# The last 16 rows of the first query weights in 31 small loads behind the first K load

## The chip, the cores and the metric

The kernel runs on one core of a Trainium2 chip. The metric is the device time of one execution in microseconds (us), as the median of several runs. A core has compute engines (TensorE for matrix products, written PE in the profile; VectorE, DVE; ScalarE, ACT; GpSimd, POOL), a queue engine that issues most of the transfers here (SyncE, SP), and 16 DMA engines that carry them out.

## The reference

One decode step of a transformer block in float32, for one token of width 512. Layer norm, 32 query heads over 8 key/value heads, a cache of 65536 positions of 128 values for each of the 8, the output projection, then a bilinear feed-forward layer of width 1792.

```python
q = (layernorm(x) @ wq).reshape(1, 1, 32, 128)          # 4 query heads for each K/V head
scores = einsum(q, repeat(k_cache, 4)) * 128 ** -0.5
o = einsum(softmax(scores), repeat(v_cache, 4))
h = x + o.reshape(1, 1, 4096) @ wo
n = layernorm(h)
out = h + ((n @ w_gate) * (n @ w_up)) @ w_down
```

The K and V caches are 537 MB of the 565 MB that the kernel reads.

## The kernel before

The work goes head by head over the 8 K/V heads (`h`). For each head the kernel needs its query weights and its output weights (512 x 512 each, both in the tile `wqo_sb`, 16 KB in each of the 128 partitions), four K blocks and four V blocks of 8.39 MB. A block is 128 partitions of 64 KB, and lies in one of two buffers, `kv[0]` and `kv[1]`, which the blocks use in turn (`buf`).

TensorE runs one loop over the heads (`head`, line 333): 16 matmuls for the query projection (L336), four K blocks of 32 matmuls (L346), the softmax with its transposes (L352 to L364), four V blocks of 32 matmuls (L374), and the projection of the output (L381, L387). A float32 matmul shows as two instructions. After the loop comes the feed-forward layer: gate and up (L409), down (L439).

SP issues all the large loads in a fixed order, written out for the eight heads. Before each K or V load from the third on it waits until TensorE has finished with the block before last, whose buffer the load takes (`done[-2]`, L132). So at most two blocks are loaded or waiting for use. The weights of the next head are loaded ahead of the third V block (L137). The weights of the first head are the first load of the program (L127, from the array `wq0`, 128 rows of 8 KB), and raise the semaphore `s_wq` by 16. TensorE waits for that semaphore once, before the loop (L331):

```python
sp.dma_start(wq_sb, wq0).then_inc(s_wq, 16)      # L127
...
take(s_wq, 16)                                   # L331
```

In the list of instructions `kv0` and `kv1` are the two buffers, `wqo_sb` the weights, `psc0` a bank of scores, `sm0` a bank for small results. ACT issues two small loads of `x` at the start (L124, L125). The last V block and the feed-forward weights come in pieces (L143, L153 to L160), and the output of 4 rows of 512 B is written at the end (L313).

Of the kernel before, what the change touches and what calls it, by code (L numbers as in the profile page):

```python
# [24 lines left out]
P = 128  # L25
# [6 lines left out]
KT = D // P  # L32
# [6 lines left out]
PE_ONLY = bass.OrderedEngineSet([mybir.EngineType.PE])  # L39
V_CUTS = (0, 16, 24, 28, 32)  # L40
U_CUTS = (0, 2, 3, 4)
D_CUTS = (0, 6, 10, 12, 13, 14)


# [15 lines left out]
def body(nc, xc, xr, kT, v, wq0, wqo, wo7, wg, wu, wd, out):  # L60
    pe_e, dve_e, act_e, pool_e, sp = nc.tensor, nc.vector, nc.scalar, nc.gpsimd, nc.sync

    def tile(name, *shape):
        return nc.alloc_sbuf_tensor(name, list(shape), F32).ap()
# [5 lines left out]
    wqo_sb = tile("wqo_sb", P, 2, KT, 512)  # L70
    wq_sb, wo_sb = wqo_sb[:, 0], wqo_sb[:, 1]
# [32 lines left out]
    def sem(name):  # L104
        sems.append(nc.alloc_semaphore(name))
        return sems[-1]
# [4 lines left out]
    s_wq, s_w = sem("s_wq"), sem("s_w")  # L111
    s_vp = [sem(f"s_vp{i}") for i in range(len(V_CUTS) - 1)]
    s_wg = sem("s_wg")
    s_wu = [sem(f"s_wu{i}") for i in range(len(U_CUTS) - 1)]
    s_wd = [sem(f"s_wd{i}") for i in range(len(D_CUTS) - 1)]
    s_x, s_xr, s_out = sem("s_x"), sem("s_xr"), sem("s_out")
# [3 lines left out]
    def pe_at(h, m):  # L120
        return M_HEAD * h + m
# [2 lines left out]
    act_e.dma_start(x_col, xc).then_inc(s_x, 16)  # L124
    act_e.dma_start(x_row, xr).then_inc(s_xr, 16)  # L125

    sp.dma_start(wq_sb, wq0).then_inc(s_wq, 16)  # L127
    done = []
    for h in range(HKV):
        for i in range(2 * NT):  # L130
            if len(done) >= 2:
                sp.wait_ge(pe.sem, done[-2])  # L132
            buf = len(done) % 2
            if i == NT + 2:
                sp.wait_ge(pe.sem, pe_at(h, M_Q))
                if h < LAST:
                    sp.dma_start(wqo_sb, wqo[h]).then_inc(s_w, 16)  # L137
                else:
                    sp.dma_start(wo_sb, wo7).then_inc(s_w, 16)
            if h == LAST and i == 2 * NT - 1:  # L140
                for p, (lo, hi) in enumerate(zip(V_CUTS, V_CUTS[1:])):
                    cs = slice(lo * 512, hi * 512)
                    sp.dma_start(kv[buf][:, cs], v[h, i - NT][:, cs]).then_inc(s_vp[p], 16)  # L143
            else:
                src = kT[h, i] if i < NT else v[h, i - NT]
                whole = i == 2 * NT - 1
                sp.dma_start(kv[buf], src).then_inc(s_vp[0] if whole else s_kv[buf], 16)
                for p in s_vp[1:] if whole else ():

                    sp.sem_inc(p, 16)  # L150
            done.append(pe_at(h, M_K + i if i < NT else M_V + i - NT))
    sp.wait_ge(pe.sem, pe_at(LAST, M_V + 2))
    sp.dma_start(wg_t, wg).then_inc(s_wg, 16)  # L153
    for p, (lo, hi) in enumerate(zip(U_CUTS, U_CUTS[1:])):
        cs = slice(lo * F, hi * F)
        sp.dma_start(wu_t[:, cs], wu[:, cs]).then_inc(s_wu[p], 16)
    sp.wait_ge(pe.sem, pe_at(LAST, M_V + 3))
    for p, (lo, hi) in enumerate(zip(D_CUTS, D_CUTS[1:])):
        cs = slice(lo * D, hi * D)
# [141 lines left out]
    for half in range(2):  # L301
        cs = slice(half * 256, min(FJ, half * 256 + 256))
# [19 lines left out]
    def take(s, n=1):  # L322
        pe_e.wait_ge(s, n).then_inc(s, -n)  # L323
# [4 lines left out]
    pe_e.wait_ge(dve.sem, c_s2)  # L328
    mm(sm[1][:, 0:1], mean_m, ln_s2, start=True, stop=True).then_inc(pre, 1)
    pe_e.wait_ge(dve.sem, c_const)  # L330
    take(s_wq, 16)  # L331

    def head():
        for r in range(REP):
# [66 lines left out]
    def project(acc, w, sems):  # L401
        for k in range(KT):
            if len(sems) == 1 and k == 0:
                pe_e.wait_ge(sems[0], 16)
            elif len(sems) > 1 and k in U_CUTS:
                pe_e.wait_ge(sems[U_CUTS.index(k)], 16)
            for j in range(4):
# [24 lines left out]
    for c in range(NC):  # L432
        if c == 8:
            pe_e.wait_ge(dve.sem, c_fp1)
        if c in D_CUTS:
            pe_e.wait_ge(s_wd[D_CUTS.index(c)], 16)
        for j in range(4):
# [46 lines left out]
```

## Time and profile before

| | us |
|---|---|
| median of 3 runs (1312.80 to 1312.94) | 1312.81 |
| the profiled execution, its own time | 1313.45 |
| its span, first to last instruction | 1312.1 |
| TensorE matmuls busy | 717.8 |
| TensorE weight loads busy | 249.1 |
| VectorE busy | 73.3 |
| ScalarE busy | 47.2 |

The mean granted clock of TensorE is 0.732 of full speed. The span is what the rows of the trace cover, and lies 1.35 us below the execution's own time. An engine's busy time is a sum over its instructions; what matters for the time is which wait ends last. For loads there are three views: the page gives the share of the 16 DMA engines' time that each queue took; a table by stretches of time gives share and GB/s; and the timeline gives the starts of matmuls, which wait for loads. In the queues' rows q1 is that of SP's transfers, q10 that of ACT's, q8 and q14 are the loads of instructions.

### The profile page before, as it was taken

The numbers are of one execution on the slowest core, as the hardware profiler recorded it, in microseconds if no ns is written. First come the engines' busy times: TensorE is split into PE (matmuls) and PEld (weight loads), VectorE is DVE, ScalarE is ACT, GpSimd is POOL, SyncE is SP. The second block draws the span as 40 slices with busy tenths as digits, with TensorE's granted clock in tenths as the row PEclk, the third lists the DMA queues.
The fourth block names the chain that finished last, engine by engine and source line by source line (L and its number), as shares of the span: only waits on it lengthen the run. The fifth ranks groups of instructions, "written<-read, shape, count | busy, mean of one in ns | idle before, by whom it ended". The sixth has DMA issues, their size and how long they took to land. (4 is left out here: it accounts for less than half of the span.)

```text
span 1312.1 us, 10526 instructions
## 1 busy us (share of the span) xinstructions
PE 717.8 (55%) x4922; PEld 249.1 (19%) x4922; DVE 73.3 (6%) x180; ACT 47.2 (4%) x102; POOL 2.5 (0%) x13
## 2 busy tenths in 40 slices
PE   4355374553755446563574736735465454645657
PEld 3011031210312112120131201312121111211213
DVE  0000000100001000010000100001000010000101
ACT  0010000100001000010000100001000010000100
POOL 0000000000000000000000000000000000000000
PEclk9777676786767867767767767668677677777677
DMA  9999999999999999999999999999999999999998
GB/s 416 436 424 446 422 440 424 440 424 440 440 428 442 426 438 426 438 428 438 440 428 440 428 438 426 438 428 438 438 432 436 430 422 441 438 428 438 438 414 356
DMA packets 12405, 564.80 MB, mean 430 GB/s; under 512 B 1510, under 2 KB 1514, under 8 KB 2155
## 3 DMA queue, kind: packets, MB, share of 16 engines
q1 hardware_dynamic: 12248, 564.67, 99.6%
q8 instruction: 6, 0.10, 0.0%
q10 hardware_dynamic: 146, 0.00, 0.0%
q14 instruction: 5, 0.03, 0.0%
HBM read 564.66 MB, written 0.00 MB: 430 GB/s over the span
## 5 line engine op out<-in xcount | busy, mean ns | idle before, releaser
L346 PE MATMUL psc<-kv,q_pad 128*32 128x512 f32 x2048 | 296.8, 744 | 257.0 <-PEq L323 257.0
L374 PE MATMUL pva<-kv,pt 128*16 128x512 f32 x2048 | 283.1, 714 | 272.9 <-PEq L323 272.7
L346 PEld LDWEIGHTS psc<-kv,q_pad 128*32 128x32 f32 x2048 | 81.6, 133 | 465.7 <-issue 465.7
L374 PEld LDWEIGHTS pva<-kv,pt 128*16 128x16 f32 x2048 | 67.5, 111 | 492.0 <-issue 492.0
L224 ACT COPY sc<-psc 128x512 f32<-128x512 f32 x32 | 18.8, 586 | 1146.2 <-PE psc L346 1146.2
L230 DVE TENSOR_REDUCE mx<-sc 128x1 f32<-128x512 f32 x32 | 21.9, 686 | 541.2 <-ACT sc L224 541.2
L336 PE MATMUL sm<-xn,wqo_sb 128*128 128x1 f32 x256 | 48.8, 325 | 2.2 <-issue 2.2
L336 PEld LDWEIGHTS sm<-xn,wqo_sb 128*128 128x128 f32 x256 | 48.1, 293 | 9.6 <-issue 9.6
L264 DVE COPY orow<-pva 128x512 f32<-128x512 f32 x8 | 5.5, 692 | 566.6 <-PE pva L374 566.6
L361 PE MATMUL ptp<-ident,sc 128*128 128x128 f32 x128 | 29.2, 395 | 10.2 <-PEq L323 9.7
L361 PEld LDWEIGHTS ptp<-ident,sc 128*128 128x128 f32 x128 | 21.3, 201 | 15.5 <-issue 14.8
L249 ACT ACTIVATE sc<-sc,nbias 128x512 f32<-128x512 f32 x32 | 22.7, 711 | 20.2 <-DVE nbias L244 20.2
L254 DVE COPY pt<-ptp 128x512 f32<-128x512 f32 x32 | 22.1, 692 | 21.5 <-PE ptp L361 21.5
L366 PE MATMUL pva<-zeros 128*32 128x512 f32 x64 | 13.8, 948 | 0.0
L387 PE MATMUL attn<-wqo_sb,o_pad 128*32 128x512 f32 x64 | 10.9, 756 | 3.3 <-PEq L323 3.3
L381 PE MATMUL sm<-sel_b,orow 128*128 128x4 f32 x64 | 8.2, 252 | 7.2 <-PEq L323 7.2
L381 PEld LDWEIGHTS sm<-sel_b,orow 128*128 128x128 f32 x64 | 7.7, 191 | 14.4 <-issue 14.4
L352 PE MATMUL sm<-ident,m 128*1 128x128 f32 x8 | 2.2, 269 | 13.7 <-PEq L323 13.7
L364 PE MATMUL sm<-l,ones 128*128 128x4 f32 x16 | 4.1, 324 | 9.6 <-PEq L323 9.6
L409 PE MATMUL psc<-kv,hn_pad 128*32 128x448 f32 x64 | 8.9, 702 | 0.6 <-DMA kv<-in_wu 0.3
L439 PE MATMUL pva<-kv,f_pad 128*32 128x128 f32 x112 | 6.1, 416 | 1.1 <-DMA kv<-in_wd 1.1
L354 PE MATMUL sm<-ones,mexp 1*128 1x1 f32 x16 | 3.3, 276 | 5.7 <-PEq L323 5.7
(83 smaller groups left out, 67.7 us busy)
## 6 DMA issues: line engine op xcount, KB each, us to landing
wqo_sb<-in_wqo SPq DMA_DIRECT2D x7, 2048.0 KB, 14.0
kv<-in_v SPq DMA_DIRECT2D x1, 4096.0 KB, 22.5
kv<-in_wg SPq DMA_DIRECT2D x1, 3584.0 KB, 18.0
kv<-in_v SPq DMA_DIRECT2D x1, 2048.0 KB, 27.0
kv<-in_v SPq DMA_DIRECT2D x2, 1024.0 KB, 30.0
kv<-in_wu SPq DMA_DIRECT2D x1, 1792.0 KB, 22.4
kv<-in_wu SPq DMA_DIRECT2D x2, 896.0 KB, 24.9
kv<-in_wd SPq DMA_DIRECT2D x1, 1536.0 KB, 20.1
```

The costliest lines, as they stand in the source:

```text
L224: copies.append(act.tick(act_e.copy(sc[s], psc[s % 2])))
L230: i = dve_e.tensor_reduce(out=mx[:, s:s + 1], in_=sc[s], axis=AX.X, op=ALU.max)
L249: act_e.activation(sc[s], sc[s], AF.Exp, bias=nbias[:, 0:1], scale=SCALE, accum_out=sums[:, s:s + 1]).then_inc(atok, 1)
L254: dve_e.tensor_copy(pt[s].rearrange("p g b h -> p b g h"), ptp[s % 2].rearrange("p (b g h) -> p b g h", b=4, h=REP)).then_inc(tok, 1)
L336: i = mm(sm[0][:, r:r + 1], wq_sb[:, k, r * P:(r + 1) * P], xn[:, k:k + 1], start=(k == 0), stop=(k == KT - 1))
L346: i = mm(psc[s % 2][32 * j:32 * j + 32, :], q_pad[:, 28 - 4 * rs:60 - 4 * rs], kv[s % 2][:, (4 * rs + j) * 512:(4 * rs + j + 1) * 512], st ...
L361: i = pe_e.transpose(ptp[s % 2][:, b * P:(b + 1) * P], sc[s][:, b * P:(b + 1) * P], ident)
L366: mm(pva[32 * j:32 * j + 32, :], zeros[:, 0:32], zeros, start=True, stop=False)
L374: i = mm(pva[32 * j:32 * j + 16, :], pt[n][:, 8 * j + rs, :, :].rearrange("p b h -> p (b h)"), vt[:, w * 512:(w + 1) * 512], start=False, ...
L381: i = mm(sm[0][:, 0:REP], orow[:, b * P:(b + 1) * P], sel_b[:, 4 * b:4 * b + 4], start=(b == 0), stop=(b == 3))
L387: i = mm(attn[32 * r:32 * r + 32, :], o_pad[:, r, :], wo_sb[:, r, :], start=True, stop=True)
L409: i = mm(acc[32 * j:32 * j + 32, :FJ], hn_pad[:, k, :], w[:, o:o + FJ], start=(k == 0), stop=(k == KT - 1))
```

## The change

The first load now brings rows 0 to 111 of the query weights. Rows 112 to 127 come in 31 loads that SP issues right behind the first K load. They go through the 2048 columns in steps of 128 (512 B of a row): in step r, from 1 to 15, one load brings the first r of the 16 rows and another the other 16-r; the last load brings the last 128 columns of all 16 rows. TensorE waits for all of them at the same place as before, for the sum of 32 loads (512).

```diff
+STEP = 128
...
-    sp.dma_start(wq_sb, wq0).then_inc(s_wq, 16)
+    flat = wqo_sb.rearrange("p a k c -> p (a k c)")
+    n_wq = 0
+    for lo, hi in ((0, P - 16),):
+        sp.dma_start(wq_sb[lo:hi], wq0[lo:hi]).then_inc(s_wq, 16)
+        n_wq += 16
...
                 sp.dma_start(kv[buf], src).then_inc(s_vp[0] if whole else s_kv[buf], 16)
                 for p in s_vp[1:] if whole else ():
                     sp.sem_inc(p, 16)
+                if not done:
+                    wq0_flat = wq0.rearrange("p k c -> p (k c)")
+                    for r in range(1, 16):
+                        cs = slice((r - 1) * STEP, r * STEP)
+                        for lo, hi in ((P - 16, P - 16 + r), (P - 16 + r, P)):
+                            sp.dma_start(flat[lo:hi, cs], wq0_flat[lo:hi, cs]).then_inc(s_wq, 16)
+                            n_wq += 16
+                    cs = slice(15 * STEP, KT * 512)
+                    sp.dma_start(flat[P - 16:, cs], wq0_flat[P - 16:, cs]).then_inc(s_wq, 16)
+                    n_wq += 16
...
-    take(s_wq, 16)
+    take(s_wq, n_wq)
```

On SP, at the start of the program, the loads stood like this before:

```order
L127 DMA wqo_sb<-in_wq0 128x2048 [waits barrier_Pool_Activation_PE_DVE_SP_release]
L147 DMA kv0<-in_kT 128x16384
L147 DMA kv1<-in_kT 128x16384
L147 DMA kv0<-in_kT 128x16384 [waits pe]
L147 DMA kv1<-in_kT 128x16384 [waits pe]
```

At the same place they now stand like this, the middle of the small loads left out:

```order
L133 DMA wqo_sb<-in_wq0 112x2048 [waits barrier_Pool_Activation_PE_DVE_SP_release]
L154 DMA kv0<-in_kT 128x16384
L163 DMA wqo_sb<-in_wq0 1x128
L163 DMA wqo_sb<-in_wq0 15x128
L163 DMA wqo_sb<-in_wq0 2x128
...
L163 DMA wqo_sb<-in_wq0 15x128
L163 DMA wqo_sb<-in_wq0 1x128
L166 DMA wqo_sb<-in_wq0 16x128
L154 DMA kv1<-in_kT 128x16384
L154 DMA kv0<-in_kT 128x16384 [waits pe]
L154 DMA kv1<-in_kT 128x16384 [waits pe]
```

Between the loads of `kv0` and `kv1` stand 31 small ones, and the wait of the third K load has not moved against its neighbours.

On TensorE, at the entry of the loop, the changed program reads:

```order
L346 MATMUL sm1<-ln_s2,mean_m 128x1 [waits dve,pool]
L408 UNCONDITIONAL_BRANCH [waits s_wq,dve]
L408 BRANCH_PREFETCH_HINT
L353 MATMUL sm0<-xn,wqo_sb 128x1 x16
L363 MATMUL psc0<-kv0,q_pad 32x512 [waits tok,s_kv0]
```

This order is that of before but for line numbers: the wait on `s_wq` stands ahead of the query projection and the first K block, and now counts loads that are queued behind that K block's own.

## Rows read from the trace of the kernel before

**Rows 1.** The page: DMA busy tenths in 40 slices; queues (packets, MB, share); bytes read.

```profile
DMA  9999999999999999999999999999999999999998
...
q1 hardware_dynamic: 12248, 564.67, 99.6%
q8 instruction: 6, 0.10, 0.0%
...
HBM read 564.66 MB, written 0.00 MB: 430 GB/s over the span
```

**Rows 2.** Busy time by stretch: 200 to 300 us, with DMA share and GB/s.

```profile
core 0: us, PE busy (x) PEld busy (x) DVE busy (x) ACT busy (x) POOL busy (x), PEclk, DMA share, GB/s
200.00:300.00 100.00, 52.28 (x349) 15.44 (x349) 6.10 (x14) 4.69 (x11) 0.00 (x0) 0.72 1.00 433
```

**Rows 3.** Timeline of TensorE: query projection and K blocks of heads 1, 2 and 8.

```profile
start us, us, engine line op out<-in xcount [idle before <-releaser]
10.40 6.97 PE L336 MATMUL sm<-xn,wqo_sb 128*128 128x1 f32 x32 [2.19 <-issue]
25.15 9.32 PE L346 MATMUL psc<-kv,q_pad 128*32 128x512 f32 x64 [7.78 <-PEq L323]
45.89 9.20 PE L346 MATMUL psc<-kv,q_pad 128*32 128x512 f32 x64 [11.42 <-PEq L323]
65.40 9.68 PE L346 MATMUL psc<-kv,q_pad 128*32 128x512 f32 x64 [10.31 <-PEq L323]
84.76 8.54 PE L346 MATMUL psc<-kv,q_pad 128*32 128x512 f32 x64 [9.68 <-PEq L323]
...
186.26 8.99 PE L346 MATMUL psc<-kv,q_pad 128*32 128x512 f32 x64 [1.72 <-PEq L323]
205.61 9.55 PE L346 MATMUL psc<-kv,q_pad 128*32 128x512 f32 x64 [10.37 <-PEq L323]
225.11 10.03 PE L346 MATMUL psc<-kv,q_pad 128*32 128x512 f32 x64 [9.96 <-PEq L323]
...
1144.45 9.46 PE L346 MATMUL psc<-kv,q_pad 128*32 128x512 f32 x64 [1.70 <-PEq L323]
1163.80 10.02 PE L346 MATMUL psc<-kv,q_pad 128*32 128x512 f32 x64 [9.89 <-PEq L323]
```

**Rows 4.** DMA packets and queues that start in 25 to 44 us, then 63 to 82.

```profile
DMA packets 140, 8.21 MB, mean 432 GB/s; under 512 B 14, under 2 KB 14, under 8 KB 14
q1 hardware_dynamic: 139, 8.19, 99.7%
q8 instruction: 1, 0.02, 0.3%
...
DMA packets 145, 8.41 MB, mean 442 GB/s; under 512 B 16, under 2 KB 16, under 8 KB 16
q1 hardware_dynamic: 144, 8.39, 102.1%
```

**Rows 5.** The chain of waits that ended last: start us, us, what.

```profile
1283.72 20.06 DMA kv<-in_wd
1303.78 0.14 issue
1303.91 6.12 PE pva L439 x112
1310.03 0.02 issue
1310.06 0.29 DVE y L311
```

**Rows 6.** DMA packets and queues of 1311.5 to 1311.8 us, the output.

```profile
DMA packets 8, 0.00 MB, mean 7 GB/s; under 512 B 4, under 2 KB 8, under 8 KB 8
q1 hardware_dynamic: 8, 0.00, 3.0%
```

**Rows 7.** The same of 1307.5 to 1308.5 us, the last rows of 2 KB.

```profile
DMA packets 37, 0.06 MB, mean 61 GB/s; under 512 B 7, under 2 KB 7, under 8 KB 37
q1 hardware_dynamic: 37, 0.06, 16.1%
```

**Rows 8.** Timeline of the issues, by SP and ACT.

```profile
0.74 0.39 SPq L127 DMA_DIRECT2D wqo_sb<-in_wq  x1
1.18 0.55 ACTq L125 DMA_DIRECT2D x_row<-in_xr  x1
1.19 0.41 SPq L147 DMA_DIRECT2D kv<-in_kT  x1
34.53 0.33 SPq L147 DMA_DIRECT2D kv<-in_kT  x1
...
1283.72 2.23 SPq L160 DMA_DIRECT2D kv<-in_wd  x5
1310.38 0.65 SPq L313 DMA_DIRECT2D out_y<-y  x1
```

**Rows 9.** Busy time by stretch, as rows 2, at the first bytes.

```profile
1.00:1.75 0.75, 0.00 (x0) 0.00 (x0) 0.15 (x2) 0.00 (x0) 0.58 (x2) 1.00 0.00 0
1.75:1.90 0.15, 0.00 (x0) 0.00 (x0) 0.00 (x0) 0.15 (x1) 0.15 (x2) 1.00 4.27 601
```

**Rows 10.** The loads of line 147: from issue to landing; first is shortest, second longest.

```profile
DMA to landing us min/median/max: 23.8/29.5/44.1
```

## The prediction

> **What bounds the kernel now.** I read the page's slices and queues first. The queue of the loads, q1, took 99.6% of the 16 DMA engines' span, and the DMA row is 9 in every slice but the last [rows 1]. So the kernel reads memory from start to end, and everything that an engine computes lies beside it. Next comes the pace. From 200 to 300 us the engines moved 433 GB/s at a busy share of 1.00 [rows 2], that is 27.06 GB/s each. The timeline of TensorE gives the same pace in loads: the K blocks of a head start 19.35 us apart (186.26 and 205.61; 1144.45 and 1163.80) [rows 3], and 8.39 MB in 19.35 us is 433.5 GB/s. The pace of the second head is that of the eighth. A block's matmuls take 8.5 to 10.0 us of those 19.35, so TensorE waits for loads, never the other way.
>
> One interval is longer: the first K block starts at 25.15 and the second at 45.89, 20.74 us later, 1.39 us over the pace [rows 3]. In that stretch the instruction queue q8 shows one packet of 0.02 MB beside the loads [rows 4]. From 63 to 82 us there is such a packet too (145 packets, 144 of them of q1 [rows 4]), yet the blocks of 65.40 and 84.76 are 19.36 apart [rows 3]. I read this so: an instruction fetch takes one DMA engine away from its loads for a while. A load counts as landed when its last engine is done. So the first fetch, which puts one engine behind the other 15, costs time, and a later one, which puts another engine behind by no more, costs none. **The end is set by the engine that is furthest behind.** At the end the chain of waits goes through the first down-projection load to 1303.78, then 6.12 us of matmuls, then the output [rows 5]. A shift of the last engine goes through to the end one for one.
>
> **The change, part by part.** *Taken away:* the last 16 rows of the first query weights as part of the first load, one row of 8 KB for each engine: 8192 B at 27.06 GB/s are 0.30 us less for every engine.
>
> *Added:* 31 loads behind the first K load. Steps of r and 16-r rows (r from 1 to 15) cover 128 columns each, a last one all 16 rows. That is 256 pieces of 512 B, the same bytes. I take it that a load of r rows gives one row to each of the first r engines. The one load of before with few rows fits: the output of 4 rows shows 8 packets, 4 of them under 512 B [rows 6], so four pieces with four completions. Then engine e (0 to 15) gets 31-2e pieces: 31 the first, 1 the last, 16 on average.
>
> *Price of a piece:* the 8 packets of the output took 3.0% of 16 engines for 0.30 us, 0.144 us, or 36 ns for a piece with its completion [rows 6]. That is a store, and mine are loads, so bounds: from below the bytes alone, 512 B at 27.06 GB/s = 19 ns; from above a row of four times the size, the 2 KB rows near the end, where 30 rows with 7 completions took 16.1% of 16 us = 2.58 us, under 86 ns each [rows 7]. I take 36, from the row of the same size. The first engine then gains 31 x 36 - 300 = +0.81 us (+0.29 to +2.4 by the bounds), the last 36 - 300 = -0.27 us, the mean +0.27. That is the stagger: 1.08 us between first and last, after the first K load, and it stays, as each queue then holds equal shares.
>
> *What the stagger buys in the long stretch:* nothing that a row shows. The stretch runs at 433 GB/s with all engines busy, and at an unchanged pace. The 1.39 us lost near the start are spread among engines in another way, not saved.
>
> *The end, then:* it moves by what the engine that is last gains. If that is the one which the first fetch hit, it lies between -0.27 and +0.81. No row names it. Several engines are hit (q8 has 6 packets [rows 1]), and the latest of several is likelier to be one with many pieces, so I take the upper part, **+0.6 us**.
>
> *Issue on SP:* 31 more instructions stand between the first and the second K load. A load of 128 rows takes 0.33 to 0.45 us (five in 2.23 us); the two loads of few rows took 0.55 (on ACT) and 0.65 (SP) [rows 8]. I take 0.65: first K issued until 1.60, 31 x 0.65 = 20.2, second K issued at 21.8. Bytes flow 1.0 us after an issue begins (0.74 to 1.75 [rows 8, 9]), so at 22.8. What hides it: the first K load lands at 1.19 + 23.8 = 25.0 [rows 10], and the pieces keep the first engine busy to about 25.8. The cover is 3.0 us; the price is nil at 0.65, and 31 us for each us of an issue above (25.8 - 1.0 - 1.6) / 31 = 0.75.
>
> *The wait of TensorE:* it now waits for all 512 counts before the first head, and so for pieces that land behind the first K load, near 25.8 and not 5. The query projection, 6.97 us, and the first K block, 9.32 [rows 3], come one after the other: 25.9 + 7.0 + 0.4 + 9.3 = 42.6. SP waits for that block before the third K load, now issued at 42.6 and not at 34.53 [rows 8], with bytes at 43.6. The second K load, which landed at 45.8 (1.6 + 44.1 [rows 8, 10]), keeps the last engine busy to about 46.4. The cover falls from 11 us to near 2.8 us, and it holds; without it each us of delay is one at the end. ScalarE and VectorE only wait longer, and are back in step by the second block at about 46.5.
>
> **A rule against the stagger.** The trace shows loads back to back at the pace of their bytes: the 8.39 MB loads 19.35 us apart [rows 3]. The Trainium skill ("DMA: Bandwidth & Descriptors", section "Rules for kernel authors") says that transfers under 64 KB pay mostly overhead and are better put together; its section "Anatomy of one DMA" gives about 2 us as the fixed part, for a load issued from GpSimd. Were that 2 us paid in turn by each of the 31 small loads, the sum by it would be 62 us, an estimate: 1374 us. The trace speaks against it, as the output's four pieces kept four engines busy for 36 ns each.
>
> **Rivals.**
> 1. *SP is too slow with the small loads* (slower). A small load would have to keep SP for over 0.75 us; the end moves by 31 times the excess. At 0.85: +0.6 + 3.2, 1316.6 us. For it: 0.65 is already twice the 0.33 of a large load, and no row shows 33 loads queued at once (SP may also have to stop until some have drained). Against: 0.65 leaves 3.0 us.
> 2. *A piece costs an engine more than 36 ns* (slower). Each 10 ns more are 0.31 us on the first engine. At the 86 ns of a 2 KB row +2.4: 1315.2; at 120 ns 31 x 0.12 - 0.3 = +3.4: 1316.2. For it: a load, not a store, and a completion behind each 512 B. Against: bytes a quarter of the 86 ns row.
> 3. *The change does not do what it says*: a load of few rows is carried by one engine. That engine has 256 x 36 ns - 0.3 = +8.9 us: 1321.7. Against it is the output with its four completions. The Trainium skill ("DMA: Bandwidth & Descriptors", section "Why a DMA increments its semaphore by 16 and not by 1") agrees: the number of engines is the largest up to 16 that divides the rows, the lowest-numbered ones.
> 4. *The 1.39 us near the start are a collision of engines in step, not the fetch*, and the stagger takes them away: 1312.8 - 1.4 = 1311.4. For it: it comes at the first interval only, when all engines have just begun together. Against: the fetch lies in the same stretch [rows 4].
> 5. *Engines in step slow each other through the whole run.* Then the pace of 19.35 us would fall; 0.1 us off each of some 67 such loads (564.67 MB / 8.39 [rows 1]) is 6.7 us: 1306. Against: 433 GB/s from the second head to the last without change, though fetches had moved engines apart by then. The Trainium skill (the same page, section "Latency and other measured facts") has copies of lock-stepped rows at large powers of two falling to half rate or less; there the sum would be far more, but no stretch here is that slow.
>
> **How the numbers follow.** The profiled run is 1313.45 with a span of 1312.1, 1.35 around it; the median of the runs is 1312.81, 0.64 below the profiled run. The shift is added to the median: 1312.81 + 0.6 = **1313.4 us**. Chances: this forecast 0.79 (alone 1312.5 to 1313.6, and to 1315.2 at the upper bound of a piece); rival 4 0.04; rival 1 0.08; rival 2 beyond its bound 0.04; rival 3 0.02; rival 5 0.03. The range takes in the forecast, the upper bound of a piece and rival 4: 1311.3 to 1315.2. Within 0.2% (2.6 us, about what a measurement of this kernel can tell from no change) are the forecast and rival 4: 0.83. Slower are rivals 1 to 3: 0.14. Faster is rival 5: 0.03.
>
> **What the profile of the changed kernel would show.** Right: the first head's query projection starts near 26 us, the first K block near 33, the second near 46.5; SP begins the second K load before 24 and the third before 44; later K blocks 19.35 us apart; 256 packets of 512 B more, and no stretch before 1280 us with a DMA share below 0.9. Wrong: a second K load issued after 24.8 (rival 1); a block pace other than 19.35 (rival 5); a second K block before 45.5 (rival 4) or beyond 48 with SP in time (rivals 2 and 3).

## The result and the profile after

| | before | after |
|---|---|---|
| median of 6 runs, us | 1312.85 (1312.72 to 1312.94) | 1319.18 (1318.98 to 1319.32) |
| ratio | | 1.0048 (95% interval 1.0038 to 1.0058) |
| span of the profiled execution | 1312.1 | 1317.9 |

The change costs 6.3 us. The forecast was 1313.4, with a range that ended at 1315.2. The page of the changed kernel gives the queues as [rows 1] do:

```profile
DMA  9999999999999999999999999999999999999998
...
q1 hardware_dynamic: 12744, 564.67, 99.6%
q8 instruction: 6, 0.10, 0.0%
...
HBM read 564.66 MB, written 0.00 MB: 428 GB/s over the span
```

The bytes are the same, and 496 more packets run on q1: 256 pieces with a completion each are 512, and the first load lost 16 rows. A slice of this page is 33 us wide, too wide to show a hole. The timeline of TensorE shows where the time went; its rows answer to [rows 3] (first the query projection, then K blocks of heads 1 and 8):

```profile
31.75 6.98 PE L353 MATMUL sm<-xn,wqo_sb 128*128 128x1 f32 x32 [24.20 <-PEq L340]
39.23 9.26 PE L363 MATMUL psc<-kv,q_pad 128*32 128x512 f32 x64 [0.50 <-PEq L340]
50.13 7.07 PE L363 MATMUL psc<-kv,q_pad 128*32 128x512 f32 x64 [1.64 <-PEq L340]
70.65 8.92 PE L363 MATMUL psc<-kv,q_pad 128*32 128x512 f32 x64 [13.45 <-PEq L340]
90.97 9.00 PE L363 MATMUL psc<-kv,q_pad 128*32 128x512 f32 x64 [11.39 <-PEq L340]
...
1151.15 9.68 PE L363 MATMUL psc<-kv,q_pad 128*32 128x512 f32 x64 [1.68 <-PEq L340]
1170.51 8.54 PE L363 MATMUL psc<-kv,q_pad 128*32 128x512 f32 x64 [9.68 <-PEq L340]
```

Against before the second block starts 4.24 us later (50.13 for 45.89), the third 5.25 (70.65 for 65.40), the fourth 6.21 (90.97 for 84.76), the first two of the last head 6.70 (1151.15 for 1144.45) and 6.71. So nearly all is lost in the first 91 us, and the long stretch keeps the pace of 19.36. The query projection starts at 31.75, where 25.9 was forecast.

The loss stays up to the last projection, whose matmuls start 6.52 us later (1310.43 for 1303.91). The spans of the two profiled executions differ by only 5.8, because these matmuls ran at different granted clocks (PEclk, third number from the end; first before, then after):

```profile
1303.90:1310.00 6.10, 6.08 (x112) 5.69 (x112) 0.00 (x0) 0.00 (x0) 0.00 (x0) 0.52 0.54 210
...
1310.40:1312.00 1.60, 1.52 (x48) 1.28 (x48) 0.00 (x0) 0.00 (x0) 0.00 (x0) 1.00 1.01 407
```

Before, all 112 ran back to back near the lower of the two levels (1.2 GHz) and ended 6.12 us after their start. In the changed kernel they ran at the upper one (2.4 GHz), waited for their loads in between, and ended 0.47 us after the last start. Why the levels differ was not tried.

The issues on SP, the counterpart of [rows 8]:

```profile
1.20 0.42 SPq L154 DMA_DIRECT2D kv<-in_kT  x1
1.67 10.19 SPq L163 DMA_DIRECT2D wqo_sb<-in_wq  x30
11.90 0.32 SPq L166 DMA_DIRECT2D wqo_sb<-in_wq  x1
12.26 0.45 SPq L154 DMA_DIRECT2D kv<-in_kT  x1
...
48.55 0.35 SPq L154 DMA_DIRECT2D kv<-in_kT  x1
```

SP is quick: 30 small loads in 10.2 us, 0.34 each, and the second K load is issued at 12.26. The third one waits for the first block's matmuls and goes out at 48.55. The busy time by stretch (columns as in [rows 2]) shows what the DMA engines do around it:

```profile
46.00:48.50 2.50, 2.50 (x24) 0.53 (x16) 0.00 (x0) 0.00 (x0) 0.00 (x0) 1.00 0.27 111
48.50:49.50 1.00, 0.00 (x0) 0.00 (x0) 0.32 (x1) 0.59 (x1) 0.00 (x0) 1.00 0.00 0
49.50:52.00 2.50, 1.87 (x20) 0.81 (x24) 0.37 (x1) 0.00 (x0) 0.00 (x0) 1.00 1.24 419
```

The share falls to 0.27, and from 48.5 to 49.5 us it is 0.00 (a packet counts where it starts). By itself this proves little: the packets are of 64 KB and start nearly together, and the kernel before has a share of 0.23 from 44 to 46 us. The completions decide. An engine ends its part of a load with a packet of under 512 B; if more work is queued, its next packet of 64 KB starts right behind. Here are the packets of before from 43.2 to 44.3 us, and those of the changed kernel from 46 to 49.5:

```profile
DMA packets 30, 0.98 MB, mean 894 GB/s; under 512 B 15, under 2 KB 15, under 8 KB 15
...
DMA packets 20, 0.28 MB, mean 80 GB/s; under 512 B 15, under 2 KB 15, under 8 KB 15
```

Before, 15 completions come with 15 new packets. In the changed kernel 15 completions come with 5 other packets: an instruction fetch, and 4 that are still of the second K load. So 15 of the 16 engines have run dry when the bytes of the third load begin to flow, at 49.5.

### The profile page after: what moved, and what is told of

The parts are those of the page before. It is cut to its first block, busy times and chain, and to the rows that moved or that the text cites. A ratio compares the mean times of both kernels' runs of the same rounds, so it can differ in the third digit from the quotient of the medians.

```text
span 1317.9 us, 10557 instructions
## 1 busy us (share of the span) xinstructions
PE 711.8 (54%) x4922; PEld 245.7 (19%) x4922; DVE 73.4 (6%) x180; ACT 47.2 (4%) x102; POOL 2.5 (0%) x13
## 5 line engine op out<-in xcount | busy, mean ns | idle before, releaser
L363 PE MATMUL psc<-kv,q_pad 128*32 128x512 f32 x2048 | 292.3, 735 | 246.9 <-PEq L340 246.9
L378 PE MATMUL ptp<-ident,sc 128*128 128x128 f32 x128 | 28.9, 392 | 10.2 <-PEq L340 9.7
L381 PEld LDWEIGHTS sm<-l,ones 128*128 128x128 f32 x16 | 3.8, 296 | 12.6 <-issue 12.6
## 6 DMA issues: line engine op xcount, KB each, us to landing
kv<-in_wu SPq DMA_DIRECT2D x2, 896.0 KB, 26.2
```

The source lines that it names most:

```text
L363: i = mm(psc[s % 2][32 * j:32 * j + 32, :], q_pad[:, 28 - 4 * rs:60 - 4 * rs], kv[s % 2][:, (4 * rs + j) * 512:(4 * rs + j + 1) * 512], st ...
L378: i = pe_e.transpose(ptp[s % 2][:, b * P:(b + 1) * P], sc[s][:, b * P:(b + 1) * P], ident)
```

## Experiments

Theory after the result: two losses on top of each other. Small loads keep an engine far longer than 36 ns, which holds up the second K load; and TensorE's late start leaves the DMA engines without work ahead of the third. Each run below stands beside runs of before on its chip (medians of 1312.76 to 1312.84).

**Without the wait.** The query weights come whole, as before; the 31 small loads go to a spare tile. Against the changed kernel:

```diff
-    for lo, hi in ((0, P - 16),):
+    for lo, hi in ((0, P),):
...
-                            sp.dma_start(flat[lo:hi, cs], wq0_flat[lo:hi, cs]).then_inc(s_wq, 16)
+                            sp.dma_start(spare[lo:hi, cs], wq0_flat[lo:hi, cs]).then_inc(s_sp, 16)
...
+    pe_e.wait_ge(s_sp, n_sp)          # after the last head
```

> The query weights come whole in the first load, as before the change, and the 31 small loads go behind the first K load into a spare tile that nothing reads (128 KB more are read, 0.3 us on average). TensorE waits for them only after the last head. So the small loads keep their cost on the DMA engines, but the query projection and the first K block start at 10 and 25 us as before, and the third K load is issued near 36 us. Theory: the change loses in two steps, completions that hold up the second K load (it lands 4.2 us later), and then engines with nothing to do between the second and the third K load, because the first K block ends at 48.5. Expected by it: the second step falls away, the time is 1317.0 (4.2 us over before) and the engines stay apart by 3 us in the long stretch. Rival, the small loads alone make the whole loss: 1319. Rival, engines that stay apart read faster: blocks less than 19.35 us apart, and a time below 1315.

Measured 1317.2 us (ratio 1.0031, 1.0020 to 1.0043). Its K blocks, second to fourth, and two of the last head:

```profile
49.84 9.02 PE L364 MATMUL psc<-kv,q_pad 128*32 128x512 f32 x64 [14.80 <-PEq L341]
69.36 9.49 PE L364 MATMUL psc<-kv,q_pad 128*32 128x512 f32 x64 [10.50 <-PEq L341]
88.71 8.36 PE L364 MATMUL psc<-kv,q_pad 128*32 128x512 f32 x64 [9.86 <-PEq L341]
...
1148.47 9.24 PE L364 MATMUL psc<-kv,q_pad 128*32 128x512 f32 x64 [1.71 <-PEq L341]
1167.82 9.81 PE L364 MATMUL psc<-kv,q_pad 128*32 128x512 f32 x64 [10.11 <-PEq L341]
```

The second block is 3.95 us later than before, the fourth still 3.95, those of the last head 4.02 (1148.47 for 1144.45). So the small loads alone cost 4 us, once (some 0.3 of it, an estimate, is for 128 KB that the kernel before does not read). The engines stayed apart: in the kept trace the 16 of them raise the semaphore for the second K load within 3.80 us, and for the third K load of the last head within 3.92 (before: 1.65 and 1.67). The pace is 19.35 all the same: this stagger changes nothing in the long stretch.

**The same with the wait.** TensorE waits for the spare loads ahead of the first head. Against the run just shown:

```diff
+    pe_e.wait_ge(s_sp, n_sp)
     take(s_wq, n_wq)
...
-    pe_e.wait_ge(s_sp, n_sp)          # after the last head
```

> As the run with the spare tile (1317.2), but TensorE waits for the small loads before the first head, as it does in the changed kernel. So the first load is that of before, and the small loads and the wait are those of the change. Theory: the wait makes the projection start near 30.7, the first K block end near 47, and the DMA engines run dry before the third K load: 1 to 1.5 us more than without the wait, 1318.2 to 1318.8, and the engines are together again after it. What is left to the 1319.2 of the changed kernel is the load of 112 rows. Rival: the late start costs nothing and the spare run's 1317.2 stays.

Measured 1319.21 us (1.0050, 1.0033 to 1.0067), 2.0 more than without the wait and the time of the changed kernel. The two sets of runs don't overlap (1318.91 to 1319.67, and 1316.59 to 1317.35). The expected range ended at 1318.8, with the rest left to the load of 112 rows; the wait takes up that rest too. K blocks, second to fourth, and the same two stretches of busy time, here and without the wait:

```profile
49.82 7.07 PE L365 MATMUL psc<-kv,q_pad 128*32 128x512 f32 x64 [1.67 <-PEq L341]
70.27 9.11 PE L365 MATMUL psc<-kv,q_pad 128*32 128x512 f32 x64 [13.38 <-PEq L341]
90.85 9.06 PE L365 MATMUL psc<-kv,q_pad 128*32 128x512 f32 x64 [11.47 <-PEq L341]
...
46.00:48.50 2.50, 2.15 (x21) 0.41 (x12) 0.00 (x0) 0.29 (x1) 0.00 (x0) 1.00 0.09 33
```

```profile
46.00:48.50 2.50, 0.00 (x0) 0.00 (x0) 0.00 (x0) 0.00 (x0) 0.00 (x0) 0.50 0.97 419
```

The second block starts where it did without the wait (49.82 and 49.84). The third is 0.9 later: that is the hole, DMA share 0.09 in place of 0.97. The fourth is 2.1 later: the interval is 20.58, not 19.35. In that stretch both kernels show one instruction fetch. The run without the wait, whose engines are apart, has:

```profile
q1 hardware_dynamic: 144, 8.39, 100.1%
q8 instruction: 1, 0.02, 0.3%
```

and loses nothing. The completions show what happens. These are the packets with the wait, from 69.1 to 69.8 us (the third load ends), 88.5 to 89.3 and 89.3 to 90.6 (the fourth):

```profile
DMA packets 32, 1.05 MB, mean 1498 GB/s; under 512 B 16, under 2 KB 16, under 8 KB 16
...
DMA packets 30, 0.98 MB, mean 1229 GB/s; under 512 B 15, under 2 KB 15, under 8 KB 15
...
DMA packets 2, 0.07 MB, mean 50 GB/s; under 512 B 1, under 2 KB 1, under 8 KB 1
```

The hole has brought all 16 engines together at the third load. At the fourth, 15 are together and one is over 1 us behind, near 90.0, and the block waits for that one. The kernel before shows the same at its second K load: 15 completions until 44.3 (above), and one alone behind:

```profile
DMA packets 2, 0.07 MB, mean 39 GB/s; under 512 B 1, under 2 KB 1, under 8 KB 1
```

So one engine falls behind in a stretch with one fetch, as the prediction read it. That it is the fetch which holds it was not tried by itself.

**The move alone.** One load of the 16 rows behind the first K load, in place of the 31 small ones.

```diff
+                    sp.dma_start(flat[P - 16:, :KT * 512], wq0_flat[P - 16:]).then_inc(s_wq, 16)
```

> The 16 rows come in one load of 16 rows behind the first K load: the move of the wait without small pieces. All theories: the projection starts near 25.6, the first K block ends near 42.3, the third K load is issued at 42.4, over 2 us before the second one has landed: no loss, 1312.5 to 1313.3. Rival, that the wait alone leaves DMA engines without work: 1314 or more, and a second block that starts after 46.5.

Measured 1317.16 us (1.0033, 1.0021 to 1.0046): a miss, for all theories. Both signs of the rival came, but not for its reason alone: the projection already started at 28.67 and not at 25.6:

```profile
28.67 6.98 PE L347 MATMUL sm<-xn,wqo_sb 128*128 128x1 f32 x32 [21.02 <-PEq L334]
36.15 9.80 PE L357 MATMUL psc<-kv,q_pad 128*32 128x512 f32 x64 [0.50 <-PEq L334]
48.34 8.77 PE L357 MATMUL psc<-kv,q_pad 128*32 128x512 f32 x64 [2.39 <-PEq L334]
67.92 9.27 PE L357 MATMUL psc<-kv,q_pad 128*32 128x512 f32 x64 [10.81 <-PEq L334]
88.75 9.10 PE L357 MATMUL psc<-kv,q_pad 128*32 128x512 f32 x64 [11.55 <-PEq L334]
```

The second block is 2.45 us late, the third 2.5, and the fourth 4.0, with an interval of 20.83. So a load of 112 rows and one of 16 cost something that no theory had. Even the first K load lands later, though less stands ahead of it. From its issue to its landing it takes, in this order, before, in the spare run, in the changed kernel and here:

```profile
kv<-in_kT SPq DMA_DIRECT2D x1, 23.8
...
kv<-in_kT SPq DMA_DIRECT2D x1, 24.8
...
kv<-in_kT SPq DMA_DIRECT2D x1, 25.5
...
kv<-in_kT SPq DMA_DIRECT2D x1, 26.2
```

The spare run has the whole first load and the 31 small ones behind, so 1.0 us comes from those; the other 0.7 of the changed kernel goes with the load of 112 rows.

**The split alone.** Both loads ahead of the first K load, nothing behind it. Against the kernel before:

```diff
-    sp.dma_start(wq_sb, wq0).then_inc(s_wq, 16)
...
+    for lo, hi in ((0, P - 16), (P - 16, P)):
+        sp.dma_start(wq_sb[lo:hi], wq0[lo:hi]).then_inc(s_wq, 16)
```

> The first load brings 112 rows, one load of 16 rows follows, and both stand ahead of the first K load; nothing stands behind it. This is the split alone. Theory S: loads of 112 rows and of the last 16 rows are slow, because engines meet where they write (in the run with one load of 16 rows behind the first K load the first K block landed 2.3 us later than before). Then the first K block starts 1.5 to 2.5 us later than the 25.15 of before and the time is near 1314.5 to 1315.5. Rival: what is slow there is the traffic behind the first K load; then the first K block starts at 25.2 and the time is 1312.5 to 1313.2.

Measured 1314.6 us (1.0015, 1.0005 to 1.0025). The first block starts at 27.58, not 25.15:

```profile
27.58 8.93 PE L353 MATMUL psc<-kv,q_pad 128*32 128x512 f32 x64 [10.80 <-PEq L330]
47.41 9.25 PE L353 MATMUL psc<-kv,q_pad 128*32 128x512 f32 x64 [10.90 <-PEq L330]
```

The same 1 MB in two loads takes 2.43 us longer. Of that 0.9 came back, since the first interval here is 19.83 and not 20.74; in the end 1.8 us are lost.

**Which rows.** Three runs put one more load, with rows of 24 KB, between the weights and the first K load, into a spare tile: the last 16 rows, 16 rows with a step of 7, and the first 112 rows.

```diff
+    sp.dma_start(spare[P - 16:], kT[0, 0][P - 16:, :6144]).then_inc(s_sp, 16)       # h1
...
+    sp.dma_start(spare[0:106:7], kT[0, 0][0:106:7, :6144]).then_inc(s_sp, 16)       # h2
...
+    sp.dma_start(spare[:P - 16], kT[0, 0][:P - 16, :6144]).then_inc(s_sp, 16)       # h3
```

> One load of 16 rows of 24 KB (rows 112 to 127 of the first K block, into a spare tile) between the weights and the first K load. Each engine gets 24 KB, 0.91 us at 27.06 GB/s. Theory S: engines that write neighbouring partitions share a way in, and the last 16 partitions have a quarter of all ways, so the load takes 3.6 us; the first K block starts 3 to 3.7 us later than before and the time is 1315.5 to 1316.5. Rival, rows don't matter: 0.9 us later, 1313.5 to 1314.

> The same with rows 0, 7, 14 to 105: 16 rows of 24 KB, spread over the partitions. Theory S: 14 of 16 ways are used, two of them twice: 0.9 to 1.8 us later, 1313.5 to 1314.7, clearly less than with the last 16 rows. Rival, rows don't matter: as with the last 16 rows.

> The same with 112 rows of 24 KB (rows 0 to 111): 7 rows for each engine, 6.4 us by bytes. Theory S: 7 rows in a row put engines onto each other's ways, and the load takes at least the 7.3 us of a way with 8 rows, likely 8 to 10 us; the time is over 1320.5. Rival, a load of 112 rows goes at the pace of one of 128: the first K block starts 6.4 us later and the time is near 1319.2.

Measured 1317.46 (1.0035, 1.0022 to 1.0049), 1314.74 (1.0014, 1.0005 to 1.0023) and 1323.84 us (1.0085, 1.0069 to 1.0100). The first K block of each, in this order:

```profile
30.40 8.66 PE L356 MATMUL psc<-kv,q_pad 128*32 128x512 f32 x64 [10.60 <-PEq L333]
```

```profile
27.35 8.79 PE L356 MATMUL psc<-kv,q_pad 128*32 128x512 f32 x64 [9.17 <-PEq L333]
```

```profile
35.80 8.85 PE L356 MATMUL psc<-kv,q_pad 128*32 128x512 f32 x64 [18.00 <-PEq L333]
```

Against 25.15 these are 5.25, 2.2 and 10.65 us, for 0.91, 0.91 and 6.36 us of bytes. The same bytes in the same number of rows cost 2.4 times as much in the last 16 partitions as spread out: the rows matter. Two things move together here, the partitions that are written and the rows of the array that are read (neighbours, or every seventh), and no run parts them. The Trainium skill ("SBUF — State Buffer", section "Door 1: The DMA port swizzle") says that groups of four partitions, with those 32 above, share one of 16 ways into the memory; by that the last 16 partitions reach 4 ways. The order of the three agrees. The sizes don't: if a way carries the 27.06 GB/s of one engine, the first would have cost 3.6 us by 4 ways, an estimate, and it cost 5.25; the 112 rows 7.3 by the busiest way, an estimate too, and they cost 10.65. So the ways may explain the order; the cost is not explained.

**Price of a small load.** The changed kernel's 256 pieces as 16 loads of 16 rows, 16 pieces for each engine:

```diff
+                    for r in range(16):
+                        cs = slice(r * STEP, (r + 1) * STEP)
+                        sp.dma_start(flat[P - 16:, cs], wq0_flat[P - 16:, cs]).then_inc(s_wq, 16)
```

> The same 16 rows in the same 256 pieces of 512 B behind the first K load, but as 16 loads of 16 rows: each engine has 16 pieces and 16 completions, none is ahead. Theory P: each engine passes its own completions one after the other, 0.18 us each (31 in 5.7 us in the changed kernel). Then 16 take 2.9 us, the query projection starts at 28.4, the third K load is issued near 45, before the second has landed: 1315 to 1316. Theory C: all completions of the core pass one place, 21 ns each (272 in 5.7 us). Then 256 take 5.4 us, the projection starts near 31.2 and the time is that of the changed kernel, 1318 to 1319. Rival, the stagger itself is what costs: then without it 1313.

Measured 1317.78 us (1.0037, 1.0023 to 1.0052), the projection at 30.34: between the two theories, 1.9 us from P and 0.9 from C. By itself this run bears out neither. But it shows that the loss needs no stagger, since here no engine is meant to be ahead. The next tells P from C for one engine. Rows 112 and 113 come in 32 loads of one row, all on the first engine, and the other 14 rows in one load:

```diff
+                    for r in range(32):
+                        lo, c = P - 16 + r // 16, r % 16
+                        cs = slice(c * STEP, (c + 1) * STEP)
+                        sp.dma_start(flat[lo:lo + 1, cs], wq0_flat[lo:lo + 1, cs]).then_inc(s_wq, 16)
+                    sp.dma_start(flat[P - 14:, :KT * 512], wq0_flat[P - 14:]).then_inc(s_wq, 16)
```

> Rows 112 and 113 come in 32 loads of one row and 128 columns, rows 114 to 127 in one load. The first engine alone has the 32 pieces, and the core has 46 completions for the 16 rows in place of 271. Theory P (0.18 us for a completion on its engine): the first engine needs 6 us for its 33, the projection starts at 31.5, the third K load is late as in the changed kernel: 1318 to 1320. Theory C (21 ns for a completion of any engine): 46 take 1 us, the first engine is 1.5 us behind by bytes and pieces, the projection starts at 26.9, the third K load is in time: 1313.5 to 1314.5.

Measured 1320.37 us (1.0056, 1.0040 to 1.0073), just above P's range, the projection at 32.43, 0.9 later than P had it and 5.5 later than C: theory P, for an engine that has the pieces alone. The DMA packets of 26.2 to 28 us in this run:

```profile
DMA packets 32, 0.34 MB, mean 189 GB/s; under 512 B 16, under 2 KB 26, under 8 KB 26
```

26 less 16 are 10 packets of 512 B, all of the first engine, in 1.8 us: **0.18 us each**, five times the 36 ns that I had. The changed kernel starts its pieces much faster at first, as the packets of 24.7 to 25.3 us show:

```profile
DMA packets 235, 0.06 MB, mean 101 GB/s; under 512 B 118, under 2 KB 235, under 8 KB 235
q1 hardware_dynamic: 235, 0.06, 47.6%
```

117 pieces with 118 completions took 47.6% of 16 engines for 0.6 us, 4.57 us: 39 ns each, the price of the prediction. So the price holds for a short run of pieces, and then an engine passes one in 0.18 us. TensorE waits for the completions, and these are slow from the start: in the kept trace of the run with single rows, 33 of them raise the semaphore about 0.18 us apart, from 26.12 to 32.07 us. In the run with 16 loads of 16 rows the last completion comes at 29.98, and the first K load, which P took to be in time, ends there at 27.21. From then on 16 pieces in 2.8 us are 0.17 each, so P's price may hold there too, behind a late K load as in the run of the move alone; as no row names the engines, this is not shown.

**Other rows, other semaphores.** The spare run with rows 0, 7 to 105 in place of the last 16 (`ps = slice(7 * lo, 7 * (hi - 1) + 1, 7)`), and the spare run with eight semaphores in turn (`.then_inc(s_sps[n_sps % 8], 16)`):

> As the run with the spare tile (whole weights first, 31 small loads behind the first K load, 1317.2), but the 16 rows are rows 0, 7, 14 to 105 instead of 112 to 127, so that the 16 engines write all over the 128 partitions. Theory P: a small load keeps an engine for 0.18 us whatever rows it writes: the second K load lands 4 us late as with the last rows, 1316.5 to 1317.3. Theory S: the small loads are slow because all of them write the last 16 partitions: then a piece costs the 36 ns of the prediction, the second K load lands 0.8 us later than before, and the time is 1313.3 to 1314.

> As the run with the spare tile (1317.2), but the small loads raise eight semaphores in turn instead of one. Theory P: the 0.18 us belong to the engine, which passes its next completion only when the one before has arrived: no change, 1316.6 to 1317.4. Rival: increments of one semaphore hold each other up; with eight the second K load lands 2 to 4 us earlier, 1313.5 to 1315.

Measured 1316.43 (1.0029, 1.0017 to 1.0040) and 1316.75 us (1.0030, 1.0019 to 1.0042), against 1317.2. Second K blocks at 49.35 and 49.93, against 49.84. Neither the rows nor a shared semaphore makes up the price; for the engine with most pieces theory P stands. What inside an engine takes the 0.18 us was not found out. In the first of the two, SP was slow: 30 small loads with a step of 7 rows took it 22.26 us, 0.74 each:

```profile
1.64 22.26 SPq L165 DMA_DIRECT2D spare<-in_wq  x30
```

**A cheap stagger.** Four loads of 8, 4, 2 and 1 rows of 8 KB into the spare tile:

```diff
+                    for r in (8, 4, 2, 1):
+                        lo = 16 - 2 * r
+                        sp.dma_start(spare[lo:lo + r], wq0_flat[lo:lo + r]).then_inc(s_sp, 16)
```

> The stagger with few completions: whole weights first, and behind the first K load four loads of 8, 4, 2 and 1 rows of 8 KB into a spare tile (120 KB more are read). The first engine gets four rows more than the last eight, 1.2 us. TensorE waits for them after the last head. Theory: the price is the extra bytes, at most 4 x 0.30 + 4 x 0.18 = 1.9 us on the first engine, and the stagger buys nothing: blocks 19.35 us apart as before, 1313 to 1314.7. Rival, the stagger was worth something and only the price of the small loads hid it: below 1312.3, by engines that are ahead when an instruction fetch takes them, or by blocks closer than 19.35 us.

Measured 1315.15 us (1.0018, 1.0009 to 1.0027), 0.45 above the range of the theory and 2.3 above before. The second block starts at 47.68, 1.79 later than before, within the 1.9 foretold; the stagger brought nothing. No run beat the kernel before.

## Why the prediction was wrong

*The bound and the long stretch: right.* Late in the run the K loads keep the pace of 19.35 us, with the engines within 1.7 us of each other (before) or 4 (the spare run), and what is lost near the start lasts until the last projection (6.5 us). Rival 5 (engines in step slow each other) is out. Rival 4 (the 1.39 us are a collision of engines in step) is out too: in that stretch of before 15 engines end together and one alone is late, and the spare run with its stagger loses the first 4 us and gains nothing back.

*The step that failed first: the price of a piece.* I took 36 ns from the four pieces of the output, with bounds of 19 and 86 ns. The 36 was well read, and 39 ns is what the first 117 pieces cost. But the output has one piece on each of four engines, and no row of before had many small loads one after the other on an engine; the 2 KB rows of my upper bound belong to loads of eight rows with one completion. The term was 31 x 36 ns = 1.1 us and is nearer 31 x 0.18 = 5.6 us. At the second K block 4 us of it show; one engine was 1.39 us behind there already, and 5.6 less 1.39 is 4.2, an estimate. Rival 2 was this mechanism, with too small a price, and the sign that the prediction gave for it came: a second K block beyond 48 (50.13) with SP in time (second K load issued at 12.26). The Trainium skill ("DMA: Bandwidth & Descriptors", section "Anatomy of one DMA") gives about 2 us as the fixed part of a load issued from GpSimd. Paid in turn, as I weighed it, that is further off on the other side: 62 us for 31 loads, an estimate, where all of the small loads cost 4.

*The step that failed second: the cover of the third K load.* I had 2.8 us left from a projection that starts at 25.9. It started at 31.75, so the first block ended at 48.49 and the third load went out at 48.55, where the forecast had 42.6; bytes at 49.5 are the 1.0 us that I had. With the cover gone, the wait cost 2.0 us (1319.21 for 1317.2). The prediction had each us beyond the cover as one at the end, which makes 48.55 - 42.6 - 2.8 = 3.1 us. The 2.0 have another make-up: 0.9 at the third block and 1.2 at the fourth, where the engines, brought together, again have one that falls behind. (The cover of before was 45.8 - 34.53 - 1.0 = 10.3 us and not 11; nothing hangs on that.)

*The step that failed third: "0.30 us less for every engine".* The first load without its last 16 rows is not shorter: with the small loads behind, the first K load lands 25.5 us after its issue, and 24.8 where the first load is whole (spare run). The split alone delays the first block by 2.43 us, and 16 rows of 24 KB in the last partitions cost far more than their bytes. In the changed kernel this term is hidden, since the run with the whole first load and the wait takes the same 1319.21: there the small loads and the hole set the time.

*The stagger itself:* I had it stay to the end. In the spare run it does; in the changed kernel the hole takes it away, as the completions of the run with the wait show. Rival 3, one engine for all pieces, is out: pieces that took 4.57 us of engine time passed in 0.6 us, on at least 8 engines.

*SP:* 0.34 us a load, not 0.65. Rival 1 is out for this kernel. With stepped rows, at 0.74, it would have been at the edge of its 0.75.

*Chances:* slower had 0.14, and 0.83 went to no change. The bounds of the piece came from one sample each, and neither sample had the pattern of the change. An upper end of some 0.2 us would have put rival 2 at over 5 us.

## What to carry to other kernels

A load's price on a DMA engine should be read from rows where loads follow each other as they will in the change; one small load on an idle engine says nothing of thirty in a row. When an engine has to wait for loads that are queued behind a long one, follow that wait to the next load which it releases: there the cover is used up. In this kernel, whose DMA engines are busy all the time at one pace, setting them apart from each other gave nothing.

## What the hardware showed that was not expected

- Small loads one after the other on one engine: 39 ns for each of the first, then 0.18 us each (10 in 1.8 us). With other rows or eight semaphores the second K load was held up about as much (3.5 and 4.0 us, for 3.95).
- One DMA engine of 16 ends its part of a load over 1 us behind the others in a stretch with one instruction fetch (the completion alone near 45.2 us before and near 90.0 with the wait); a block waits for it, unless another engine is further behind (in the spare run the interval stayed 19.35).
- Rows matter to a load: 16 rows of 24 KB cost 5.25 us for rows 112 to 127 and 2.2 us when spread, for 0.91 us of bytes. 112 rows of 24 KB cost 10.65 us for 6.36.
- The time that SP needs for a load differs with its rows: 0.34 us for 1 to 15 neighbouring rows, 0.49 for each of 16 loads of 16 rows, 0.74 with a step of 7. In the run with single rows, the load of 14 rows of 8 KB kept it for 7.20 us, which is not explained:

```profile
12.87 7.20 SPq L165 DMA_DIRECT2D wqo_sb<-in_wq  x1
```
